# A second layer of 15 products on 2x3x3 blocks, from the ninth output tile on

## The chip, the cores and the metric

One core of a Trainium2 chip runs the whole program. The time is device microseconds (us) of that core; the kernel before takes 1906.94 us, the median of three runs (1906.71 to 1906.95). Engines: PE multiplies matrices into PSUM; VectorE (DVE), ScalarE (ACT) and GpSimd (POOL) do the rest; SyncE (SP) starts transfers. Each engine takes its instructions strictly in the order in which the program holds them, and waits where an input or a buffer is not ready.

## The reference

```python
def reference(x, w_in, w_out):                  # x: (8, 3008, 256) fp32
    X = np.fft.fft(np.fft.fft(x, axis=1), axis=2).real.astype(np.float32)
    h = X.reshape(24064, 256) @ w_in            # w_in: (256, 2048)
    g = np.where(h > 0, h, np.exp(np.minimum(h, 0)) - 1)
    return (g @ w_out).astype(np.float32)       # w_out: (2048, 256)
```

A Fourier transform over sequence and channels, of which the real part is kept, feeds a two-layer network with the activation ELU. Everything is float32.

## The kernel before

The real part of the transform has two mirrored halves, so the kernel works on 12032 columns (rows of the output, transposed), each of which yields two output rows: a "plus" and a "minus" one. The columns are cut into 47 tiles of 256. For a tile and each of 8 steps (`i`), the first layer forms two blocks of 128 hidden channels (`f = 2i, 2i+1`) in a bank `H` of PSUM: `seed` (ACT) puts a rank-one term there, `mm_P` adds the cosine part (2 products), `even_part` (ACT) copies that to `E`, `mm_Q` adds the sine part (2 products). `H` is then the plus side, and `h_minus` (DVE) makes the minus side `2E-H`. ELU takes, for each side, `below` and `exp` on ACT and `elu` (`g_plus`, `g_minus`) on DVE. The results stand in a buffer `G` of one step.

The second layer multiplies `w_out` with these. `sum_1` to `sum_4` (POOL, 256 columns each) and the summed weights `WT` turn the 8 products of a 2x2 by 2x2 block product into 7 (`mm_X1`, `mm_X2`, `mm_X3`) of 256 columns, which accumulate over the tile's 8 steps in four banks, `pA` to `pD`. Per tile four DVE additions (`comb_1`, `comb_2`, `comb_22`, `comb_3`) and an ACT copy (`comb_copy`) rebuild the result, two DVE transposes turn it, and SP stores it. The bank `M` holds the negative part of the minus side. A product is two matmul instructions in the trace, each with its own weight load: fp32 goes through PE in two parts.

Beside this runs the Fourier transform of the next batch element. A batch element spans 47 steps. Its folds and turns are POOL and DVE additions in SBUF (`mirror_sum`, `half_sum`, `channel_fold`, `quarter_pairs`, `turn_pairs`), its matrix products are short (`Quarter.mms`, 94 or 95 columns), use `H` banks too, and DVE unfolds them into rings `Rr` and `Ir` that the first layer reads.

The order is written by hand: each operation is entered with a time (`at(t, fn)`, in steps of `PERIOD`), all are sorted by it, and the recorded order on each engine follows. The times are not kept by the chip; only the order is. The three `H` banks are given out by `bank_H` by those times. A last small part, `mid_*`, computes the one output row of each batch element that the halves leave out; its products with `w_out` stand at the program's end.

Of the kernel before, what the change touches and what calls it, by code (L numbers as in the profile page):

```python
# [177 lines left out]
def kernel(  # L178
# [184 lines left out]
    ebias = cpool.tile([128, 1], FP, tag="ebias")  # L363
    nc.vector.memset(ebias, -896.0 * 2.0**23)
    wide = moe_w_in.dtype == I64
    assert moe_w_out.dtype == moe_w_in.dtype
# [173 lines left out]
        for c in range(8)  # L540
    ]

    MC = {}
    for kodd in range(2):
        for ri in range(2):
# [10 lines left out]
            )  # L556

    QM = {}

    def load_quarter_mats(ri, kodd):  # L560
        t = cpool.tile([128, BW], FP, tag=f"MC{ri}{kodd}", name=f"QM{ri}{kodd}")
        QM[ri, kodd] = t
        n = sum(QW[i % 2] for i in range(2 * ri + kodd))
# [6 lines left out]
    warm = cpool.tile([128, 1], FP, tag="warm")  # L570
# [55 lines left out]
    def vtt(o, a, b, op):  # L626
        pin(nc.vector.tensor_tensor(out=o, in0=a, in1=b, op=op))
# [651 lines left out]
    def ext_side(g, rows=NB):  # L1279
        kodd, par = EXT[g]  # L1280
        n = NO if kodd else NE if par else 2 * NH
        t = spool.tile([128, 384], FP, tag="side", bufs=2, name="side")
        act(t[0:rows, 0:n], state["ext"][32 * g : 32 * g + rows, 0:n])
        state["side", par] = t

# [104 lines left out]
    def even_part(i):  # L1390

        S = steps[i]
        S.E = spool.tile([128, 512], FP, tag="E", bufs=2, name="E")
# [12 lines left out]

    def open_G(S):
        if not hasattr(S, "G"):
            S.G = spool.tile([128, GW], FP, tag="G", bufs=3, name="G")

    def h_minus(i):
        S = steps[i]
        open_G(S)
        pin(
            nc.vector.scalar_tensor_tensor(  # L1415
                out=two(S.G[:, 0:512])[:, :, ::-1], in0=two(S.E), scalar=2.0,
                in1=two(S.H), op0=ALU.mult, op1=ALU.subtract,
            )
        )

    def below(o, h):

# [33 lines left out]
    def g_minus(i):  # L1456
        S = steps[i]
        elu(S.G[:, 0:512], S.G[:, 0:512], S.M)

    def blk(S, j, n=1):  # L1460
        return S.G[:, j * TW : (j + n) * TW]

    def tt_of(i):

        return vtt if i == n_tiles * 8 - 1 else gtt

    def sum_1(i):
        S = steps[i]
# [1 line left out]

    def sum_3(i):
        S = steps[i]
        tt_of(i)(blk(S, 4), blk(S, 2), blk(S, 0), ALU.subtract)

    def sum_2(i):
        S = steps[i]
        tt_of(i)(blk(S, 2), blk(S, 5), blk(S, 0), ALU.subtract)

    def sum_4(i):
        S = steps[i]  # L1480
        tt_of(i)(blk(S, 6), blk(S, 2), blk(S, 1), ALU.add)

    def prod(i, a, half, lhsT, j):
        S, T = steps[i], tiles[i // 8]
# [56 lines left out]

    def comb_copy(q):
        T = tiles[q]
        T.p1 = spool.tile([128, TW], FP, tag="p1", bufs=1, name="p1")
        act(T.p1, T.acc[0][:, 0:TW])

    def plain_v(q):
# [36 lines left out]
        store(q, 0, 1, 0)  # L1584
        store(q, 1, 0, 1)

    def turn_half(q, part):

        T = tiles[q]
        if not part:  # L1590
            T.o = spool.tile([128, 1024], FP, tag="ot", bufs=2, name="ot")
        src = (T.v if part > 1 else T.u)[:, part % 2 * TW : (part % 2 + 1) * TW]
        pin(nc.vector.transpose(out=T.o[:, part * TW : (part + 1) * TW], in_=src))
        store(q, part, *((1, 0), (0, 1), (0, 0), (1, 1))[part])

    def comb_half(q, half):
        T = tiles[q]
        c = slice(half * TW, (half + 1) * TW)
        vtt(T.v[:, c], T.v[:, c], T.acc[3][:, c], ALU.add)

    def turn_v(q):
        T = tiles.pop(q)
        tiles[q, 1] = T
# [6 lines left out]
    def store(q, part, sg, half):  # L1610

        T = tiles[q]
        j, end = q * TW, min((q + 1) * TW, n_cols)
        while j < end:
            b, c = divmod(j, HALF)
            odd, cc = divmod(c, RUN)
# [32 lines left out]


    def mid_mm():
        pm = state["mid"] = bank_H(now[0] + 3 * PERIOD, True)
        for n, (W, R) in enumerate(((Wc, R4), (Ws, Rx4))):
            wv = W.rearrange("p (j g a) -> p g j a", g=4, a=32)
            for g in range(4):
                mm(pm[32 * g : 32 * g + 32, :], R, wv[:, g], n == 0, n == 1)

    def mid_below():
        t = spool.tile([128, HALF + 1], FP, tag="rx", bufs=1, name="mid")
        state["mh"], state["mr"] = t[:, 0:512], t[:, 512:1024]  # L1660
        below(state["mr"], state["mid"])

    def mid_g():
        h, r = state["mh"], state["mr"]
        elu(h, state["mid"], r)
        pin(nc.vector.transpose(out=r, in_=h))

    def mid_out():
        po = state["mo"] = bank_H((total + 2) * PERIOD + 2.8)
        t = state["mr"]  # L1670
        for j in range(NF):
            g = j % 4
            mm(
                po[32 * g : 32 * g + 32, 0:ND],
                t[:, 32 * j : 32 * j + 32],
                w2[:, j * ND : (j + 1) * ND],
                j < 4,
                j >= 12,
            )

    def mid_copy():
        act(state["mh"][:, 0:ND], state["mo"][:, 0:ND])

    def mid_pick():
        po = state["mo"] = bank_H((total + 3) * PERIOD)
        mm(po[0:32, 0:ND], pick[:, 0:32], state["mh"][:, 0:ND], True)

    def mid_store():
        ob = state["mr"][0:NB, 0:ND]
        pin(nc.vector.tensor_copy(out=ob, in_=state["mo"][0:NB, 0:ND]))  # L1690
        nc.sync.dma_start(
            out=bass.AP(
                tensor=out.tensor,
                offset=out.offset + HALF * ND,
                ap=[[SEQ * ND, NB], [1, ND]],
            ),
            in_=ob,
        )

    state = {}  # L1700
# [189 lines left out]
    for i in range(8):  # L1890
        at((12.9 + 0.5 * i) * T + 3.6, lambda i=i: sum_weights(i))
    total = n_tiles * 8
    WINOGRAD = (
        (T + 2.91, sum_1),
        (T + 3.6, sum_3),
# [2 lines left out]
        (2 * T + 0.87, mm_X1),  # L1898
        (2 * T + 3.04, mm_X2),
    )  # L1900
    for slot in range(total):
        i = slot % 2 * 8 + slot // 2 if slot < 16 else slot
        t = slot * T

        X3 = (
            (
                3 * T + 0.1 if i % 8 == 0 else 3 * T + 3.045 if i == total - 2 else 2 * T + 3.05,
                "",
                mm_X3,
            ),  # L1910
# [37 lines left out]
    for q in range(2, n_tiles):  # L1948
        t = (8 * q + 9) * T
        if q == n_tiles - 1:  # L1950
            turns = (
                (4.205, lambda q: turn_half(q, 0)),
                (T + 2.4, lambda q: turn_half(q, 1)),
                (T + 2.5, lambda q: comb_half(q, 0)),
                (T + 2.6, lambda q: turn_half(q, 2)),
                (T + 2.7, lambda q: comb_half(q, 1)),
                (T + 2.8, lambda q: turn_half(q, 3)),
            )
        else:
# [126 lines left out]
    for b in range(2, NB):  # L2086
# [62 lines left out]
    last = total - 40  # L2149
    at(  # L2150
        (last - 8) * T,
        lambda: nc.sync.dma_start(out=Rx4[127:128, 0:NB], in_=r4_dr),
    )
    for n, dt, fn in (
        (last, 4.75, mid_mm),
        (last + 1, 1.46, mid_below),
        (last + 2, 1.6, lambda: exp_neg(state["mr"])),
        (last + 3, 1.0, mid_g),
        (total + 1, 3.3, mid_out),
        (total + 2, 2.75, mid_copy),  # L2160
        (total + 2, 2.91, mid_pick),
        (total + 2, 2.92, mid_store),
    ):
        at(n * T + dt, fn)
    for t, _, fn in sorted(events, key=lambda e: e[:2]):
# [32 lines left out]
```

## Time and profile before

| what | value |
|---|---|
| median of three runs | 1906.94 us |
| the profiled execution | 1907.16 us |
| its span, first to last instruction | 1905.4 us (1.8 us lie around it) |
| granted PE clock | 1.000 |
| busy: PE, DVE, ACT, POOL | 1898.3, 1232.0, 1391.4, 1353.1 us |

The span is one row after another of PE's work. Busy times count an instruction from its start to its end, and PE's instructions overlap, so the distance of their starts is what a product costs. Stretches differ: those with much of the transform's DVE work (about 640 to 760 us, and again every 235 us), those with less, and the end without any.

### The profile page before, as it was taken

What the parts mean: (1) busy time and instruction counts of PE and PEld (TensorE: products, weight loads), DVE (VectorE), ACT (ScalarE), POOL (GpSimd) and SP (SyncE); (2) the same over time, 40 slices, a digit from 0 to 9 for tenths busy, and PEclk for the clock granted to TensorE, in tenths of its full rate; (3) what the DMA queues carried; (4) which work ended last, traced back from release to release, by engine and by line L of the source; (5) the groups of instructions that cost most, each with busy time, mean ns of one, the idle gap of its engine ahead of it and who ended that gap; (6) DMA issues with size and microseconds to landing.
All of it is one profiled execution on the core that took longest, in us unless ns stands there. A gap on an engine that the chain in (4) does not pass through costs nothing.

```text
span 1905.4 us, 28620 instructions
## 1 busy us (share of the span) xinstructions
PE 1898.3 (100%) x8972; PEld 1656.8 (87%) x8972; DVE 1232.0 (65%) x2174; ACT 1391.4 (73%) x2803; POOL 1353.1 (71%) x1846
## 2 busy tenths in 40 slices
PE   9999999999999999999999999999999999999999
PEld 6888888888888888888888888888888888888887
DVE  8755555667666676667766677666776667655445
ACT  5767667777777777777777777777777777777775
POOL 4888658786687766777667777687766777556664
PEclk9999999999999999999999999999999999999999
DMA  8145211211011110211102111022110210100101
GB/s 340 45 33 43 55 24 45 53 24 36 12 44 41 32 33 12 47 40 30 31 19 50 35 27 31 13 56 44 24 24 16 55 21 15 17 12 15 20 11 24
DMA packets 278901, 73.66 MB, mean 39 GB/s; under 512 B 254382, under 2 KB 268972, under 8 KB 278750
## 3 DMA queue, kind: packets, MB, share of 16 engines
q1 hardware_dynamic: 270110, 61.40, 15.9%
q0 software_dynamic: 6464, 10.18, 1.7%
q8 instruction: 71, 1.16, 0.3%
q14 instruction: 80, 0.66, 0.1%
q10 hardware_dynamic: 2176, 0.26, 0.1%
HBM read 46.92 MB, written 24.80 MB: 38 GB/s over the span
## 4 chain that ended last, share of the span: by engine, by line
PE 96%; DVE 2%; ACT 1%; issue 0%; DMA 0%; POOL 0%; ACTq 0%; POOLq 0%; DVEq 0%
PE H L621 37%; PE pB L621 17%; PE pD L621 17%; PE pC L621 17%; PE pA L621 9%; DMA xl<-in_x_dram,ix 0%; DVE e L721 0%; ACT G L633 0%; DVE o L721 0%; POOL w L630 0%; DVE G L1431 0%; DVE E L1401 0%; ACT M L633 0%; ACT E L633 0%; DVE pow L462 0%
## 5 line engine op out<-in xcount | busy, mean ns | idle before, releaser
L630 POOL TENSOR_TENSOR G<-G 128x256 f32<-128x256 f32 x1437 | 1047.4, 737 | 498.0 <-DVE G L1431 358.5
L1431 DVE SCALAR_TENSOR_TENSOR G<-G,H 128x512 f32<-128x512 f32 x376 | 258.2, 687 | 554.5 <-ACT G L633 554.5
L633 ACT ACTIVATE G<-H 128x512 f32<-128x512 f32 x376 | 224.5, 597 | 259.0 <-DVE G L1415 255.4
L621 PE MATMUL H<-Rr,Wsc 128*128 128x256 f32 x1504 | 388.7, 381 | 1.0 <-ACT Wsc L633 0.5
L621 PE MATMUL H<-Ir,Wsc 128*128 128x256 f32 x1504 | 386.7, 380 | 0.7 <-DVE E L1401 0.7
L633 ACT ACTIVATE H<-Rb,wex 128x256 f32<-128x256 f32 x720 | 341.2, 474 | 40.0 <-DVE G L1431 21.5
L621 PE MATMUL pC<-G,WT 128*128 128x256 f32 x1440 | 369.8, 379 | 0.0
L633 ACT ACTIVATE E<-H 128x512 f32<-128x512 f32 x360 | 214.5, 596 | 182.0 <-PE H L621 181.7
L621 PEld LDWEIGHTS H<-Ir,Wsc 128*128 128x128 f32 x1504 | 285.6, 190 | 40.6 <-DVE E L1401 1.5
L621 PEld LDWEIGHTS H<-Rr,Wsc 128*128 128x128 f32 x1504 | 281.7, 190 | 43.1 <-issue 2.3
L621 PEld LDWEIGHTS pC<-G,WT 128*128 128x128 f32 x1440 | 274.2, 190 | 36.6
L1415 DVE SCALAR_TENSOR_TENSOR G<-E,H 128x512 f32<-128x512 f32 x376 | 255.0, 678 | 8.4 <-PE H L621 4.3
L1431 DVE SCALAR_TENSOR_TENSOR G<-M,G 128x512 f32<-128x512 f32 x376 | 256.7, 683 | 0.7 <-ACT M L633 0.7
L633 ACT ACTIVATE G<-G 128x512 f32<-128x512 f32 x376 | 235.0, 625 | 0.0
L621 PE MATMUL pA<-G,w 128*128 128x256 f32 x784 | 229.6, 380 | 0.1
L621 PE MATMUL pB<-G,w 128*128 128x256 f32 x784 | 229.5, 379 | 0.0
L621 PE MATMUL pD<-G,w 128*128 128x256 f32 x784 | 229.4, 379 | 0.0
L633 ACT ACTIVATE M<-G 128x512 f32<-128x512 f32 x376 | 224.4, 597 | 2.8 <-DVE G L1415 2.8
L633 ACT ACTIVATE M<-M 128x512 f32<-128x512 f32 x376 | 222.7, 592 | 0.1
L621 PE MATMUL pB<-G,WT 128*128 128x256 f32 x720 | 214.7, 380 | 0.0
L621 PE MATMUL pD<-G,WT 128*128 128x256 f32 x720 | 214.4, 379 | 0.0
L621 PEld LDWEIGHTS pA<-G,w 128*128 128x128 f32 x784 | 149.2, 190 | 20.6 <-DVE G L1431 0.5
(175 smaller groups left out, 1794.3 us busy)
## 6 DMA issues: line engine op xcount, KB each, us to landing
out_dram<-ot SPq DMA_DIRECT2D x496, 32.0 KB
xq<-in_x_dram SPq DMA_DIRECT2D x48, 94.0 KB
out_dram<-ot SPq DMA_DIRECT2D x256, 2.0 KB
Rb<-r SPq DMA_DIRECT2D x10, 376.0 KB
raw<-in_moe_w_in_dram SPq DMA_DIRECT2D x7, 512.0 KB
MC<-dft_mats SPq DMA_DIRECT2D x3, 943.5 KB
xq<-in_x_dram SPq DMA_DIRECT2D x12, 192.0 KB
xq<-in_x_dram SPq DMA_DIRECT2D x36, 64.0 KB
```

Of the source, the lines that this page charges most:

```text
L621: nc.tensor.matmul(out_, lhsT=lhsT, rhs=rhs, start=start, stop=stop, skip_group_check=True)
L630: pin(nc.gpsimd.tensor_tensor(out=o, in0=a, in1=b, op=op))
L633: pin(nc.scalar.activation(out=o, in_=i, func=func, **kw))
L1415: nc.vector.scalar_tensor_tensor(out=two(S.G[:, 0:512])[:, :, ::-1], in0=two(S.E), scalar=2.0, in1=two(S.H), op0=ALU.mult, op1=ALU.subtract,)
L1431: nc.vector.scalar_tensor_tensor(out=o, in0=e, scalar=-1.0, in1=h, op0=ALU.add, op1=ALU.max)
```

## The change

The first 8 tiles stay. From the ninth on (`NEW = 8`, 39 tiles) the second layer works on other blocks:

- The 512 columns of a hidden block (256 minus, 256 plus) lie side by side in a ring `GG` of 8 such blocks. Its first and last column are set aside (`keep_ends`, four small DVE copies per tile); the 510 left are three runs of 170 (`BL`).
- Three hidden blocks make a group; five groups and one single block are the 16. A group is a product of 2x3 weight blocks with 3x3 column blocks, 18 products done as 15 with sums. The single block takes 6. So a tile has 81 products of 170 columns where it had 56 of 256. They accumulate in five banks: `pA` to `pD` and `M`, three regions in each.
- Per group 8 sums stand ahead of the products (`group_sum`): `A1` to `A4`, `S3`, `S4` on POOL, `S1`, `S2` on DVE, some over 340 columns at once. The single block has two (POOL).
- 37 summed weight blocks (`make_combo`) are made once, in steps 61 to 70, by turns on POOL and DVE; they lie in free parts of buffers of the transform and in the old `WT`.
- The outputs take 19 operations per tile (`out_sum`): 15 on DVE, 2 on ACT, 2 on POOL, in place of four on DVE and one on ACT.
- `below_minus` now writes into `H` in place of `M`, so that an `H` bank is held until `g_minus`. `E` has one buffer from that tile on.
- The columns set aside, with those of `mid`, are 86 (`NS`) and take 16 products of 256 columns at the end (`single_mm`) and one store; the `mid` products at the end go.
- Each operation of a tile has its own time in a table `TILE_AT`, the same for all 39 tiles. The transform's times stay.

```diff
+NEW = 8
+BL = 170
+NS = 2 * (NP - NEW) + 8
...
+    def new_below_minus(i):
+        S = steps[i]
+        below(two(S.H), S.m)
...
+    def keep_ends(i):
...
+        pin(nc.vector.tensor_copy(out=o, in_=b[:, :, 0:512:511]))
...
+        tt = vtt if name in ON_DVE else gtt
+        if name == "A1":
+            tt(F(0, 1), B(7, 5), B(8, 6), ALU.add)
+        elif name == "A2":
+            tt(F(2, 1), F(0, 1), B(5, 8), ALU.add)
+        elif name == "A3":
+            tt(F(6), B(0), B(2), ALU.add)
+        elif name == "S1":
+            tt(F(4, 3), B(0, 2), B(1, 6), ALU.subtract)
+        elif name == "A4":
+            b3 = B(3)
+            tt(F(5, 6), F(4, 6), pair_of(b3, 0), ALU.add)
+        elif name == "S2":
+            tt(F(4, 7), F(4, 5), B(6, 4), ALU.subtract)
+        elif name == "S3":
+            tt(F(0), B(2), F(0), ALU.subtract)
+        elif name == "S4":
+            tt(F(7), F(7), F(2), ALU.subtract)
+
+    ON_DVE = ("S1", "S2")
...
+            W = wblock((g,), WPLAIN[p]) if p in WPLAIN else wcombo((g,), p)
+            M = gb(g, PLAIN[p]) if p in PLAIN else fb(5 * (q - NEW) + g, FORM[p])
+        mm(region(p), W, M, not g and j % 3 == 0, g == 5)
...
+        if name == "D0":
+            act(tmp(2), R(9))
+        elif name == "D1":
+            vtt(cb(u, 0), tmp(2), R(11), sub)
+        elif name == "D2":
+            vtt(tmp(0), R(8), tmp(2), sub)
...
+        elif name == "E5":
+            gtt(cb(u, 0, 2), cb(u, 0, 2), tmp(1, 2), add)
...
+        elif name == "E7":
+            vtt(cb(v, 1), cb(v, 1), cb(v, 0), add)
+        elif name == "E8":
+            vtt(cb(v, 0, 2, 2 * BL), cb(v, 0, 2, 2 * BL), regions(7, 15), add)
...
+    def single_mm(f):
+        if not f:
+            state["single"] = bank_H((total + 30) * PERIOD)
+        mm(
+            state["single"][0:NS, 0:ND],
+            single(f),
+            w2[:, f * ND : (f + 1) * ND],
...
+    TILE_AT = {
+        "seed": (
+            -3.840, -0.624, 2.855, 5.507, 15.632, 16.480, 23.562, 26.176,
...
+        t = 61.0 + 0.25 * n
...
+        at(t * T + 1.3, lambda gs=gs, p=p, n=n: make_combo(gs, p, gtt if n % 2 else vtt))
+    for q in range(NEW, n_tiles):
+        new_tile(q)
...
-    for slot in range(total):
+    for slot in range(8 * NEW):
```

What the order becomes is shown at three places. First PE in a tile of the steady part, where `H<-Rr` and `H<-Ir` are the first layer's products and `p...<-G` those of the second. Before:

```order
L621 MATMUL H<-Rr,Wsc 128x256 x2
L621 MATMUL pA<-G,w_68 128x256
L621 MATMUL pB<-G,w_68 128x256
L621 MATMUL pB<-G,WT_903 128x256
L621 MATMUL H<-Ir,Wsc 128x256 x2
L621 MATMUL pC<-G,WT_904 128x256
L621 MATMUL pC<-G,WT_902 128x256
L621 MATMUL pD<-G,WT_905 128x256
L621 MATMUL pD<-G,w_68 128x256
L621 MATMUL H<-Rr,Wsc 128x256 x2
```

Now, with `GG` the ring, `F` the sums, and `QM_...`, `WT_...` the weight sums:

```order
L639 MATMUL H<-Rr,Wsc 128x256 x2
L639 MATMUL pD<-GG,QM_2548 128x170
L639 MATMUL M<-GG,QM_2312 128x170
L639 MATMUL pC<-F,QM_2452 128x170
L639 MATMUL pD<-F,QM_2452 128x170
L639 MATMUL pA<-GG,WT_875 128x170
L639 MATMUL pD<-F,QM_2548 128x170
L639 MATMUL H<-Ir,Wsc 128x256 x2
L639 MATMUL pC<-F,w_68 128x170
L639 MATMUL pA<-GG,QM_2452 128x170
L639 MATMUL M<-F,QM_2548 128x170
L639 MATMUL M<-GG,w_68 128x170
```

The regular round of 4 and 7 products per step is gone: products of several groups are mixed, and more of them stand between two parts of the first layer.

Second, DVE where it also has the transform's half sums (`xq<-xq,xq`). Before (L1431 `elu`, L1415 `h_minus`):

```order
L1415 SCALAR_TENSOR_TENSOR G<-E,H 128x2x256
L627 TENSOR_TENSOR xq_11050<-xq_11042,xq_11110 96x256 x2
L1431 SCALAR_TENSOR_TENSOR G<-G,H 128x512
L1431 SCALAR_TENSOR_TENSOR G<-M,G 128x512
L1415 SCALAR_TENSOR_TENSOR G<-E,H 128x2x256
L627 TENSOR_TENSOR xq_11118<-xq_11042,xq_11110 96x256 x2
L1431 SCALAR_TENSOR_TENSOR G<-G,H 128x512
```

Now, in such a place of the new part (L1455 `elu`, L1488 `new_h_minus`; `F<-GG` and `GG<-GG` of 2x170 are `S1`, those of 340 `S2`; a group's sums lie in `F` or in the ring's tail by turns):

```order
L1455 SCALAR_TENSOR_TENSOR GG<-H,GG 128x2x256
L1488 SCALAR_TENSOR_TENSOR GG<-EE,H 128x2x256
L645 TENSOR_TENSOR xq_6476<-xq_6580,xq_6660 94x256 x2
L645 TENSOR_TENSOR GG<-GG 128x340
L645 TENSOR_TENSOR F<-GG 128x2x170
L1455 SCALAR_TENSOR_TENSOR GG<-GG,H 128x2x256
L1488 SCALAR_TENSOR_TENSOR GG<-EE,H 128x2x256
L1526 COPY SS<-GG 128x4x2
L1455 SCALAR_TENSOR_TENSOR GG<-GG,H 128x2x256
L645 TENSOR_TENSOR xq_6543<-xq_6580,xq_6660 94x256 x2
L645 TENSOR_TENSOR F<-F,GG 128x340
```

Sums of two SBUF operands now stand between the activations on DVE, beside the transform's own.

Third, PE at the program's end. Before:

```order
L621 MATMUL pC<-G,WT_902 128x256
L621 MATMUL pD<-G,WT_905 128x256
L621 MATMUL pD<-G,w_68 128x256
L621 MATMUL pD<-G,WT_905 128x256
L621 MATMUL pD<-G,w_68 128x256
L621 MATMUL H<-w_68,mid 32x256 x16
L621 MATMUL H<-mid,pick 32x256
```

Now:

```order
L639 MATMUL pD<-GG,WT_878 128x170
L639 MATMUL pD<-F,WT_877 128x170
L639 MATMUL M<-GG,WT_875 128x170
L639 MATMUL pD<-GG,WT_875 128x170
L639 MATMUL M<-F,WT_878 128x170
L639 MATMUL H<-w_68,SS 86x256 x12
L639 MATMUL H<-w_68,CC 86x256 x4
L639 MATMUL M<-WT_875,w_68 128x170 x2
L639 MATMUL pD<-WT_875,w_68 128x170
```

The 16 products of the columns set aside come ahead of the last tile's last three products, and nothing of `mid` comes behind them.

More of the change, by code (lines that the diff above doesn't have):

```diff
@@ L1392, in even_part @@
         S = steps[i]
-        S.E = spool.tile([128, 512], FP, tag="E", bufs=2, name="E")
+        S.E = next_of("E", EE, 512, 1 if i >= 8 * NEW else 2)
         if S.seeded:
@@ L1458, in g_minus, with new_h_minus, new_below_plus, new_exp_plus @@
         elu(S.G[:, 0:512], S.G[:, 0:512], S.M)
+    def new_h_minus(i):
+        S = steps[i]
+        S.m, S.p = slots(i)
+        pin(
+            nc.vector.scalar_tensor_tensor(
+                out=S.m[:, :, ::-1], in0=two(S.E), scalar=2.0,
+                in1=two(S.H), op0=ALU.mult, op1=ALU.subtract,
+            )
+        )
+    def new_below_plus(i):
+        S = steps[i]
+        S.m, S.p = slots(i)
+        below(S.p, two(S.H))
+    def new_exp_plus(i):
+        exp_neg(steps[i].p)
@@ new lines, in out_tiles, with cb, tmp @@
+    def out_tiles(q):
+        T = tiles[q] = Tile()
+        if "uv" not in state:
+            state["uv"] = [
+                spool.tile([128, 512], FP, tag=t, bufs=1, name=t) for t in "uv"
+            ]
+            for t in state["uv"]:
+                pin(nc.vector.memset(t[:, 0:512:511], 0.0))
+        T.u, T.v = state["uv"]
+    def cb(t, n, m=1, step=BL):
+        v = t[:, 1 + BL * n : 1 + BL * (n + 1)]
+        return v if m == 1 else pair_of(v, step)
+    def tmp(n, m=1):
+        v = EE[:, 512 + BL * n : 512 + BL * (n + 1)]
+        return v if m == 1 else pair_of(v, BL)
@@ L1460, in blk, with new_turn @@
+    def new_turn(q, part):
+        T = tiles[q]
+        if not hasattr(T, "o"):
+            T.o = spool.tile([128, 1024], FP, tag="ot", bufs=2, name="ot")
+        c = 512 * part
+        pin(nc.vector.transpose(out=T.o[:, c : c + 512], in_=(T.u, T.v)[part]))
+        store(q, 2 * part, 1, part)
+        store(q, 2 * part + 1, 0, part)
     def blk(S, j, n=1):
         return S.G[:, j * TW : (j + n) * TW]
-    def tt_of(i):
-        return vtt if i == n_tiles * 8 - 1 else gtt
     def sum_1(i):
@@ L1585, in turn_u @@
         store(q, 1, 0, 1)
[L1587 to L1599, printed above, removed]
     def turn_v(q):
@@ L1893 @@
+    at((total + X0 + 1) * T, single_store)
     WINOGRAD = (
```

360 lines of the change are left out of this document (305 added, 55 removed), and 9 rows, old and new, of the table TILE_AT.

## The prediction

> **What bounds the kernel now.** I read the page's busy times and chain first, then windows, then shapes and the timeline where a price was needed.
>
> ```profile
> PE 1898.3 (100%) x8972; PEld 1656.8 (87%) x8972; DVE 1232.0 (65%) x2174; ACT 1391.4 (73%) x2803; POOL 1353.1 (71%) x1846
> ...
> PE 96%; DVE 2%; ACT 1%; issue 0%; DMA 0%; POOL 0%; ACTq 0%; POOLq 0%; DVEq 0%
> ```
>
> PE never rests, and the chain that ended last is PE for 96%. So less PE work is worth its full length as long as nobody else becomes late. Three windows show who could: one with much of the transform on DVE, one with less, one with none.
>
> ```profile
> core 0: us, PE busy (x) PEld busy (x) DVE busy (x) ACT busy (x) POOL busy (x), PEclk, DMA share, GB/s
> 640.00:760.00 120.00, 120.00 (x589) 106.51 (x588) 85.68 (x167) 87.95 (x180) 82.92 (x116) 1.00 0.12 25
> 758.00:875.00 117.00, 117.00 (x543) 103.24 (x543) 73.57 (x114) 88.41 (x179) 92.62 (x126) 1.00 0.18 40
> 1740.00:1880.00 140.00, 140.00 (x650) 123.55 (x649) 69.06 (x112) 105.51 (x210) 85.36 (x119) 1.00 0.09 14
> ```
>
> DVE is busy for 71%, 63% and 49%: the transform takes 22 points of it in the first.
>
> **PE's gain.** What a product costs is the distance of two starts.
>
> ```profile
> 1606.78 0.60 PE L621 MATMUL pD<-G,WT 128*128 128x256 f32 x2
> 1607.21 0.59 PE L621 MATMUL pD<-G,w 128*128 128x256 f32 x2
> 1607.64 0.36 PE L621 MATMUL H<-QM,e 95*128 95x95 f32 x2
> 1607.84 0.39 PE L621 MATMUL H<-QM,o 94*128 94x95 f32 x2
> 1608.06 0.39 PE L621 MATMUL H<-QM,e 94*128 94x95 f32 x2
> 1608.29 0.39 PE L621 MATMUL H<-QM,o 94*128 94x94 f32 x2
> 1608.51 1.06 PE L621 MATMUL H<-Rr,Wsc 128*128 128x256 f32 x4
> ```
>
> A product of 256 columns takes 0.432 us (0.43 from start to start), one of 94 or 95 takes 0.22. For 170 I need the slope, from the shapes' mean times:
>
> ```profile
> L621 PE MATMUL pA<-G,w 128*128 128x256 f32 x784 | 229.6, 380 | 0.1
> L621 PE MATMUL H<-MC,eo 128*128 128x376 f32 x16 | 5.7, 479 | 0.0
> L621 PE MATMUL H<-MC,eo 128*128 128x188 f32 x8 | 1.6, 323 | 0.0
> L621 PEld LDWEIGHTS H<-QM,e 94*128 94x128 f32 x192 | 27.2, 192 | 1.2
> ```
>
> From 188 to 256 columns an instruction grows by 57 ns, from 256 to 376 by 99: 0.83 ns a column both times. So 170 columns take 86 x 0.83 = 71 ns less than 216, that is 145 ns, and a product 0.289 us. Below that the short products show a floor of 0.11 us per instruction, which 145 ns clears. Per tile 56 x 0.432 = 24.2 us become 81 x 0.289 = 23.4: 0.8 us, over 39 tiles 31 us. With the first layer's 32 products (13.8) a tile then asks 37.2 us of PE.
>
> Those short products also judge a rule. The Trainium skill, "Trainium Kernel Development and Optimization", section Best Practices, says to judge distance to roofline by LDWEIGHTS busy time, not by matmul busy time. By the 190 ns that a load lasts, the change, with 50 more loads per tile, would make PE the slower; that is the third rival below. The rows differ: four loads of 192 ns each went by in 2 x 0.22 us, so a load's duration is not what it blocks.
>
> **The program's end.**
>
> ```profile
> 1898.91 0.60 PE L621 MATMUL pD<-G,w 128*128 128x256 f32 x2
> 1899.44 1.93 PE L621 MATMUL H<-w,mid 128*32 128x256 f32 x32
> 1902.11 0.62 PE L621 MATMUL H<-mid,pick 128*32 128x256 f32 x2 [0.74 <-ACT mid L633]
> 1903.20 0.29 SPq L1691 DMA_DIRECT2D out_dram<-mid  x1
> ```
>
> The 16 new products take 16 x 0.432 = 6.9 us of PE; 1.93 + 0.62 = 2.5 go: +4.4. Behind PE's last second-layer product stood some 6 us (1899.5 to 1905.4: `mid`, its copies, its store). Now, after `x13` and `x7` of the single block, DVE's chain E2, E4, E6, E7, E8 and two transposes stand there, near 3.5 us by the rows below, and a store: the same length. The last tile has no next tile's first layer to fill PE while its last sums are made: +1 (0 to +3).
>
> **DVE, the cover that may fail.** The prices:
>
> ```profile
> L627 DVE TENSOR_TENSOR u<-p,pB 128x512 f32<-128x512 f32 x45 | 30.6, 681 | 0.4 <-PE pB L621 0.4
> L627 DVE TENSOR_TENSOR u<-v,pC 128x256 f32<-128x256 f32 x45 | 18.9, 420 | 1.5
> L627 DVE TENSOR_TENSOR xq<-xq,xq 96x256 f32<-96x256 f32 x48 | 37.5, 817 | 0.0
> L627 DVE TENSOR_TENSOR Rr<-bs,H 128x376 f32<-128x376 f32 x2 | 1.0, 542 | 1.0 <-PE H L621 1.0
> L627 DVE TENSOR_TENSOR bs<-H,anti 128x188 f32<-128x188 f32 x3 | 1.0, 348 | 3.4 <-ACT anti L633 3.4
> L627 DVE TENSOR_TENSOR R<-bs,H 128x1 f32<-128x1 f32 x7 | 1.0, 149 | 0.0
> L1431 DVE SCALAR_TENSOR_TENSOR G<-G,H 128x512 f32<-128x512 f32 x24 | 16.4, 685 | 24.4 <-ACT G L633 24.4
> ```
>
> The last row is that of the window 640 to 760: 24 steps, three tiles of 40 us, so a tile there has 85.68 / 3 = 28.6 us of DVE. In the end window a tile (38 us) has 0.49 x 38 = 18.6. The transform's share in a busy tile is thus 10.0, in a lighter one (0.63 x 38 = 23.9) 5.3.
>
> Of the 18.6 the old sums go: three of 0.68 and one of 0.42, less overlap, 2.4. What comes:
> - S1, S2, ten per tile, 340 columns, both operands in SBUF. Alone 0.51 (between 348 ns for 188 and 542 for 376). The half sums, which are of this kind, take 817 ns for 256 columns where 420 is the price with one operand in PSUM. So up to 0.90 for 340. I take 0.70: 7.0 (5.1 to 9.0).
> - 13 output sums of 170 from PSUM and E7: 14 x 0.33 = 4.6. E8 (340): 0.5.
> - Four copies of 8 elements: 0.15 each by the one-column row, up to 0.4 if they wait: 0.8.
>
> 18.6 - 2.4 + 12.9 = 29.1 us per tile (27 to 32). PE gives it 37.2 in the end part: ample. In a lighter tile it is 34.4 of 37.2. In a busy tile it is 39.1, and PE there needs 40 - 0.8 = 39.2: level. That is the place that decides. A queue at its limit loses time, but what waits for DVE has some room: after `mm_Q`, the next use of that `H` bank needs `h_minus`, `below_minus`, `exp_minus`, `g_minus` and two `seed`s, and PE's order puts its own work between. The prices are the 685 ns above and these:
>
> ```profile
> L633 ACT ACTIVATE M<-G 128x512 f32<-128x512 f32 x376 | 224.4, 597 | 2.8 <-DVE G L1415 2.8
> L633 ACT ACTIVATE H<-Rb,wex 128x256 f32<-128x256 f32 x720 | 341.2, 474 | 40.0 <-DVE G L1431 21.5
> ```
>
> That is 2 x 0.69 + 2 x 0.6 + 2 x 0.47 = 3.5 us; the fifth step's `mm_P` stands some 6 us of PE work behind the third's `mm_Q` (counted in the new order), so 2 to 2.5 us are left. The first products of a group have more. I take 0.4 us lost per busy tile (0 to 2), 120 us in each 235 us, six times, 18 tiles: 7 us. Lighter tiles: none (0 to 0.5 each).
>
> **POOL and ACT.**
>
> ```profile
> L630 POOL TENSOR_TENSOR G<-G 128x256 f32<-128x256 f32 x1437 | 1047.4, 737 | 498.0 <-DVE G L1431 358.5 <-PE H L621 82.0
> L630 POOL TENSOR_TENSOR WT<-w 128x128 f32<-128x128 f32 x16 | 7.8, 485 | 0.0
> L630 POOL TENSOR_TENSOR o<-e,o 94x384 f32<-94x384 f32 x12 | 12.0, 997 | 0.0
> L633 ACT ACTIVATE p<-pA 128x256 f32<-128x256 f32 x45 | 17.1, 379 | 1.6 <-PE pA L621 1.6
> ```
>
> POOL's 32 x 0.737 = 23.6 per tile become 16 of 340 (0.91) and 18 of 170 (0.57), 24.8; with the transform's 4 (82.92 / 3 less 23.6) 29 of 39: hidden. ACT loses one copy of 0.38 and gets two of about 0.3: hidden at 105.5 / 140 = 75%. `below_minus` into `H` instead of `M` costs the same 597 ns; what it holds longer is the bank, counted above. SP's queue loses and gains a few stores: nothing. The 37 weight sums, about 13 us of DVE and POOL each within 43 us of a busy stretch where both already run at 70%, fill both up: +2 (0 to +4).
>
> How POOL and DVE disturb each other is to be read from four POOL sums without and with two half sums beside them:
>
> ```profile
> 1891.05 3.02 POOL L630 TENSOR_TENSOR G<-G 128x256 f32<-128x256 f32 x4 [1.74 <-DVE G L1431]
> ...
> 762.59 3.15 POOL L630 TENSOR_TENSOR G<-G 128x256 f32<-128x256 f32 x4 [0.80 <-DVE G L1431]
> ...
> 763.56 1.60 DVE L627 TENSOR_TENSOR xq<-xq,xq 96x256 f32<-96x256 f32 x2
> ```
>
> POOL loses 0.13 us to two DVE sums; DVE pays 1.60 for 0.84. So it is DVE that pays.
>
> **Sum** against the profiled execution's 1907.2 us (0.2 above the median): 1907.2 - 31 + 4.4 + 1 + 2 + 7 = 1890.6, say 1890.
>
> **Rivals.**
> 1. No stall: DVE's S sums near 0.51, 37 us in a busy tile. 1907.2 - 31 + 4.4 + 1 = 1882. For it: PE idles nowhere before; against it: DVE's sum without room. Chance 0.30.
> 2. Slower: DVE becomes the bound in the busy tiles, since each S waits out POOL's running sum (0.90), each copy too. Then 32 + 10 = 42 against 39.2: 2.8 x 18 = 50, so 1932. It decides from 1882 + 25, that is 1.4 us per busy tile, or 40.6 us of DVE. For it: the half sums' 817 ns. Against: in busy tiles POOL rests for 31%, and S2 follows a POOL sum that has just ended. Chance 0.22. The Trainium skill, "SBUF — State Buffer", section Who interferes with whom, has two SBUF operands on DVE and POOL's reads exclude each other for whole instructions, which speaks for it; by the trace POOL loses far less than that.
> 3. The weight load rules PE: 226 loads x 0.190 = 42.9 us per tile against 38.0 now, x 39 = +191, near 2100. The 0.22 us pitch speaks against it. Chance 0.02.
> 4. It doesn't do what it says: losses of 22 to 29 us eat the gain, within 0.2% (3.8 us, about what a measurement of this kernel can tell from no change): a mild form of 2. Chance 0.12.
> 5. The likeliest, the sum above, with 3 to 20 us of stalls: 1884 to 1902. Chance 0.34.
>
> Faster: 0.30 + 0.34 - 0.02 for its upper edge = 0.62; same 0.12; slower 0.26 with that edge and 3. Range 1873 to 1928: below, a gain of 37 (170 columns in pure proportion to 256: 0.287) and no loss at the end; above, most of rival 2. The likeliest's own range is 1876 to 1903.
>
> **What would show it.** In the trace after: matmuls of 170 columns 145 ns apart (right) or 190 (rival 3); S1, S2 at 0.6 to 0.8 us on DVE (0.9 and more: rival 2); PE's busy share in windows like 640 to 760 at 97 to 100%, its idle there put down to DVE; POOL under 80%. I am wrong if PE idles in the end window, where DVE has 8 us to spare, since then the order itself, a bank or a ring slot, makes PE wait.

## The result, and the profile after

The changed kernel takes 1927.5 us (median; 1926.85 to 1927.9), the kernel before 1906.95: a ratio of 1.0106 (1.0088 to 1.0123). It is some 20 us slower where 17 us faster was forecast. The time lies at the upper edge of the stated range (1873 to 1928), but that edge stood there for another cause, rival 2, so that it lies inside is luck. Its profiled execution took 1927.36 us, with a span of 1925.6.

The page's busy times, the summary of the chain that ended last, and PE's two largest waits:

```profile
PE 1884.2 (98%) x10920; PEld 1744.3 (91%) x10920; DVE 1553.0 (81%) x3165; ACT 1441.3 (75%) x2843; POOL 1362.2 (71%) x1945
...
PE 84%; DVE 10%; ACT 2%; issue 1%; POOL 1%; DMA 1%; ACTq 0%; SPq 0%; DVEq 0%; POOLq 0%
...
PE pD L639 <- DVE v L645: 11.4, 5, 2.3
PE H L639 <- ACT EE L651: 4.4, 4, 3.1
```

PE's share of the chain fell from 96% to 84%, and DVE now holds 10%. PE's own work did shrink. Laid end to end at the distances that their starts show (144 ns for 170 columns, 216 for 256, the short ones at their floor of 110), PE's instructions come to 1894.1 us before (1.9 of it the `mid` products) and 1867.1 after: 27.0 less. The rest is told by the starts of PE's instructions, what each leaves open beyond its price, summed by stretch:

| where the time went, us | before | after | difference |
|---|---|---|---|
| PE's instructions end to end | 1894.1 | 1867.1 | -27.0 |
| PE open in the first 360 us | 2.8 | 5.1 | +2.3 |
| PE open at 360 to 480 us (old order meets new) | 0.1 | 8.9 | +8.8 |
| PE open around five places (588, 822, 1058, 1294, 1530 us, 20 us to each side) | 0.0 | 19.7 | +19.7 |
| PE open elsewhere | 4.3 | 7.8 | +3.5 |
| from PE's last instruction to the span's end | 3.0 | 15.8 | +12.8 |
| sum | | | +20.1 |

The windows of the changed kernel, with the same columns as before: the busy stretch, one of the five places, and the end part.

```profile
640.00:760.00 120.00, 119.69 (x746) 114.06 (x745) 107.02 (x243) 92.21 (x185) 84.56 (x126) 1.00 0.13 25
...
800.00:840.00 40.00, 37.61 (x216) 35.15 (x215) 32.53 (x58) 28.41 (x55) 26.89 (x41) 0.96 0.18 37
1800.00:1840.00 40.00, 40.00 (x243) 37.78 (x242) 30.68 (x65) 32.25 (x63) 24.14 (x37) 1.00 0.09 15
```

Where DVE is fullest (107 of 120) PE loses 0.3 us in 120. It loses 2.4 in 40 where DVE has 7 to spare. So the loss in the steady part isn't DVE's load. One row of DVE and the POOL rows beside it show what it is, at the second of the five places:

```profile
820.75 3.97 DVE L645 TENSOR_TENSOR v<-v 128x170 f32<-128x170 f32 x1
824.64 0.68 DVE L1455 SCALAR_TENSOR_TENSOR GG<-H,GG 128x512 f32<-128x512 f32 x1
...
820.42 0.81 POOL L648 TENSOR_TENSOR u<-u,EE 128x170 f32<-128x170 f32 x1
821.19 1.64 POOL L648 TENSOR_TENSOR F<-F,GG 128x340 f32<-128x340 f32 x2
822.80 0.48 POOL L648 TENSOR_TENSOR GG<-GG 128x170 f32<-128x170 f32 x1
823.24 0.79 POOL L648 TENSOR_TENSOR u<-u,EE 128x340 f32<-128x340 f32 x1
823.98 0.54 POOL L648 TENSOR_TENSOR F<-GG,F 128x170 f32<-128x170 f32 x1
```

`E7` (`v<-v`, 170 columns), one of the output sums, lasts 3.97 us and ends when POOL, which ran six sums without a pause, has stopped. `E8` stands behind it on DVE, and the next tile's first `pD` product on PE needs `E8`. The view of the buffer `v` gives least, median and greatest duration (ns) over all 39 tiles:

```profile
L645 DVE TENSOR_TENSOR v<-pA,EE x39: 329/329/331, 421.2 to 1900.9; 128x170 f32<-128x170 f32 x39
L645 DVE TENSOR_TENSOR v<-v x39: 320/325/3973, 430.9 to 1910.8; 128x170 f32<-128x170 f32 x39
```

The sum with an operand in PSUM (`pA`) hardly varies, though POOL runs beside 38 of its 39. `E7`, with both operands in SBUF, takes some 325 ns in 33 tiles, 0.65 us in the last and 3.97 us in five.

Why five tiles, and not all, can be read from a tile without the loss:

```profile
862.16 0.50 DVE L645 TENSOR_TENSOR GG<-GG 128x340 f32<-128x340 f32 x1
862.58 0.32 DVE L645 TENSOR_TENSOR v<-v 128x170 f32<-128x170 f32 x1
...
861.32 0.55 POOL L648 TENSOR_TENSOR u<-u,EE 128x170 f32<-128x170 f32 x1
862.83 1.66 POOL L648 TENSOR_TENSOR GG<-GG 128x340 f32<-128x340 f32 x2 [0.96 <-DVE GG L645]
```

Here `E3` (POOL, `u<-u,EE` of 170 columns) has ended, POOL waits for DVE's group sum, and `E7`, which stands right behind that sum, gets in before POOL starts again. It is so in all 33 tiles: POOL idles as `E7` starts. In the five, 1.2 us of the transform's sums (`xq<-xq,xq`) stand on POOL just ahead of `E3`, `E3` still runs as `E7` starts, and the sums behind it start without a wait.

### The profile page after: what moved, and what is told of

Same layout as the page of the kernel before. It is cut to its first block, busy times and chain, and to the rows that moved or that the text cites. A ratio compares the mean times of both kernels' runs of the same rounds, so it can differ in the third digit from the quotient of the medians.

```text
span 1925.6 us, 34720 instructions
## 1 busy us (share of the span) xinstructions
PE 1884.2 (98%) x10920; PEld 1744.3 (91%) x10920; DVE 1553.0 (81%) x3165; ACT 1441.3 (75%) x2843; POOL 1362.2 (71%) x1945
## 4 chain that ended last, share of the span: by engine, by line
PE 84%; DVE 10%; ACT 2%; issue 1%; POOL 1%; DMA 1%; ACTq 0%; SPq 0%; DVEq 0%; POOLq 0%
PE H L639 33%; PE pD L639 12%; PE pC L639 11%; PE pB L639 10%; PE pA L639 9%; PE M L639 9%; DVE v L645 2%; DVE GG L1455 2%; ACT H L651 1%; DVE EE L645 1%; DVE CC L1526 1%; ACT GG L651 1%; DVE GG L1488 1%; DVE GG L645 1%; DVE e L929 0%
## 5 line engine op out<-in xcount | busy, mean ns | idle before, releaser
L648 POOL TENSOR_TENSOR GG<-GG 128x340 f32<-128x340 f32 (+2 forms) x774 | 547.1, 718 | 306.3 <-DVE GG L645 138.7
L1455 DVE SCALAR_TENSOR_TENSOR GG<-GG,H 128x512 f32<-128x512 f32 x376 | 256.8, 683 | 124.7 <-ACT GG L651 119.6
L651 ACT ACTIVATE EE<-H 128x512 f32<-128x512 f32 x360 | 213.4, 593 | 174.3 <-PE H L639 122.8
L651 ACT ACTIVATE GG<-H 128x512 f32<-128x512 f32 x376 | 223.7, 595 | 159.4 <-PE H L639 71.6
L1488 DVE SCALAR_TENSOR_TENSOR GG<-EE,H 128x512 f32<-128x512 f32 x312 | 212.6, 682 | 86.3 <-PE H L639 47.4
L1455 DVE SCALAR_TENSOR_TENSOR GG<-H,GG 128x512 f32<-128x512 f32 x312 | 212.4, 685 | 69.2 <-ACT H L651 64.4
L651 ACT ACTIVATE GG<-GG 128x512 f32<-128x512 f32 x376 | 235.8, 627 | 8.5
L648 POOL TENSOR_TENSOR F<-F,GG 128x340 f32<-128x340 f32 x196 | 164.2, 850 | 79.1 <-DVE F L645 77.2
L651 ACT ACTIVATE H<-GG 128x512 f32<-128x512 f32 x312 | 185.3, 594 | 41.6 <-DVE GG L1455 39.7
L651 ACT ACTIVATE H<-H 128x512 f32<-128x512 f32 x312 | 179.7, 576 | 4.6
```

Source lines behind the costliest of these rows:

```text
L648: pin(nc.gpsimd.tensor_tensor(out=o, in0=a, in1=b, op=op))
L651: pin(nc.scalar.activation(out=o, in_=i, func=func, **kw))
L1455: nc.vector.scalar_tensor_tensor(out=o, in0=e, scalar=-1.0, in1=h, op0=ALU.add, op1=ALU.max)
L1488: nc.vector.scalar_tensor_tensor(out=S.m[:, :, ::-1], in0=two(S.E), scalar=2.0, in1=two(S.H), op0=ALU.mult, op1=ALU.subtract,)
```

## The experiments

The kernel before ran beside each and took 1906.9 to 1907.0 us. Ratios are to it.

| edit of the changed kernel | median us | ratio (95% interval) |
|---|---|---|
| none | 1927.5 | 1.0106 (1.0088 to 1.0123) |
| E7 on POOL | 1913.0 | 1.0032 (1.0020 to 1.0045) |
| set-aside products last | 1923.9 | 1.0090 (1.0073 to 1.0107) |
| weight sums spread | 1927.4 | 1.0108 (1.0091 to 1.0125) |
| all three | 1909.2 | 1.0012 (1.0003 to 1.0022) |
| E7 with an operand in PSUM | 1966.1 | 1.0310 (1.0294 to 1.0326) |
| longer POOL run beside E7 | 1919.6 | 1.0065 (1.0049 to 1.0080) |
| whole stores | 1927.3 | 1.0109 (1.0094 to 1.0125) |
| PSUM operand, whole stores, shorter end | 1960.1 | 1.0279 (1.0265 to 1.0293) |
| pause behind E3 | 1911.8 | 1.0026 (1.0017 to 1.0036) |
| pause, whole stores, shorter end | 1907.05 | 0.9998 (0.9989 to 1.0007) |
| the same, three queues evenly | 1904.8 | 0.9988 (0.9979 to 0.9997) |
| the same, weight sums on POOL | 1908.0 | 1.0008 (0.9999 to 1.0017) |

**E7 on POOL.**

```diff
-            vtt(cb(v, 1), cb(v, 1), cb(v, 0), add)
+            gtt(cb(v, 1), cb(v, 1), cb(v, 0), add)
```

> Only E7 (one sum of 170 columns, both operands in SBUF) moves from DVE to POOL. In the trace after, E7 lasts 3.97 us five times, once per batch element, while POOL runs six sums without a gap; PE then waits 2.45 us for E8 and its clock falls to 0.5 for some us. Theory (the shared port keeps E7 out): the five waits and the cold clock behind them go, 5 x (2.45 + 2) = 22 us, so about 1906 us, granted clock 1.00 from 500 to 1880 us. Rival (DVE and the order are too loaded there, E7 is only where it shows): a wait of like length turns up behind another DVE or POOL operation, and the time stays within 6 us of 1927.5.

All five waits for `v` are gone and the time fell by 14.5 us, less than the 22 of the theory. A new wait came up, the longest near 833 us:

```profile
PE pC L639 <- POOL GG L648: 2.4, 2, 2.0
```

**The set-aside products last.** (`X0` is their time in the order, in steps.)

```diff
-X0 = 2.6
+X0 = 3.6
```

> Only the 16 products of the columns set aside and their store move behind the last tile's last three products. Theory (the end chain E2 to the last store waits 7 us behind them on PE): the last transposes start 7 us earlier; but 27 stores of the set-aside rows then share the queues with the 32 of the tile, so 4 to 7 us are won: 1921 to 1924 us. Rival (the end is set by the issue of the stores, not by PE): within 1.5 us of 1927.5.

3.6 us less, within what was expected. The 6.9 us of products no longer stand ahead of the last tile's last three, but the span still ends 12 us behind PE: the stores remain.

**The weight sums spread.**

```diff
-        t = 61.0 + 0.25 * n
-        if gs[0] == 3:
-            t = max(t, 66.5 + 0.15 * (n - 24))
+        t = 57.2 + 0.35 * n
+        if gs[0] >= 3:
+            t = 66.5 + 0.25 * (n - 24)
```

> Only the 37 weight sums are entered over 57.2 to 69.5 steps in place of 61 to 70: the first 24 start earlier and lie farther apart. In the trace after, PE loses 8 us between 360 and 440 us, where it lost nothing before. Theory (the sums crowd DVE and POOL there): 3 to 7 us are won, 1920 to 1924 us. Rival (what is lost there is the new order meeting the old at the eighth tile, whatever the sums do): within 1.5 us of 1927.5.

No change in time. PE's longest wait in the transition fell from 3.1 to 1.3 us, but the stretch from 320 to 440 us still lost 7.0 us in place of 8.3.

**All three together.**

> The three edits together. If they cost independently, their gains add: 22 + 5 + 5, so about 1895 us, below the 1906.9 of before. If the waits only move, the time stays above 1907.

1909.2, far from the 1895 expected: 18.3 us of the 20 are back. The gains do add (14.5 + 3.6 + 0.1); each was smaller than expected.

**E7 with an operand in PSUM.**

```diff
+    def v0_to_psum(q):
+        act(region(14), cb(tiles[q].v, 0))
...
-            vtt(cb(v, 1), cb(v, 1), cb(v, 0), add)
+            vtt(cb(v, 1), cb(v, 1), R(14), add)
...
+        at(t0 + 58.9, lambda: v0_to_psum(q))
```

> E7 stays where it stands on DVE, but one of its two operands now comes from PSUM: ACT copies E6's result into the region of product 14, which is free by then (one more ACT operation of 0.3 us per tile), and E7 adds from there. Nothing else changes. Theory: what keeps E7 out for 3.97 us is that both its operands lie in SBUF while POOL runs six sums without a gap; with one in PSUM it takes 0.33 us in all five places, PE's five waits of 2.45 us go, and with them the clock's dips: 1927.4 - 14.4 (what E7 on POOL saved) = 1913, 1910 to 1915. Rival: E7 waits there for something else in its place of the order, a result or a semaphore; then it lasts 3.97 us again and the time stays at 1927.

Half right. `E7` lasted 332 to 334 ns in every tile, and POOL was running as it began in 38 of the 39. But the time rose to 1966, because the cure made a wait of its own:

```profile
DVE v L645 <- ACT pD L651: 81.9, 39, 3.9
PE pD L639 <- DVE v L645: 46.7, 38, 1.5
```

ACT's copy stands in ACT's order behind work that waits for PE. `E7` waits for it 2.1 us in every tile, and PE for `E8` 1.2 us in 38. The operand is what decides, but one more engine in a chain that PE waits for cost some 54 us (1966.1 less the 1911.8 of the pause below) where some 15 were won.

**A longer POOL run beside E7.**

```diff
             gtt(cb(u, 0, 2), cb(u, 0, 2), tmp(1, 2), add)
+            if q in (12, 18, 24, 30, 36):
+                for n in range(2):
+                    gtt(tmp(0, 2), pair_of(w2[:, 0:BL], BL), pair_of(w2[:, 512 : 512 + BL], BL), add)
```

> E7 as in the changed kernel, but in tiles 12, 18, 24, 30 and 36 alone POOL makes two sums more of 340 columns (of weights, into a buffer nobody reads) between E5 and S3, inside its run without a gap. Theory: DVE gets in only where POOL pauses, so E7 lasts as much longer as the run: 3.97 + 2 x 0.82 = 5.6 us in five places, PE's wait there grows from 2.45 to about 4.1, five times 1.65 plus a longer time at the low clock: 1934 to 1940. Rival: DVE's stay is set by something of fixed length (4 us), or POOL lets DVE in after a fixed number of sums; then E7 lasts 3.97 and the time is 1927 to 1929.

Neither: `E7` got shorter and the kernel 7.9 us faster. PE's five waits are 1.95 us in place of 2.45, and no fall of its clock follows them (see the end).

```profile
819.62 3.47 DVE L645 TENSOR_TENSOR v<-v 128x170 f32<-128x170 f32 x1
...
822.12 0.78 POOL L648 TENSOR_TENSOR u<-u,EE 128x340 f32<-128x340 f32 x1
822.97 1.89 POOL L648 TENSOR_TENSOR EE<-w 128x340 f32<-128x340 f32 x2
```

The sums that I added write where `E5` had read, so the first of them waits for `E5`'s end. In the records POOL's sums otherwise start some 34 ns before the one ahead has ended; here 78 ns lie between (end at 833.483, start at 833.561 in the trace's own clock, which is 822.896 and 822.974 from the span's start). `E7` came in at that pause, one POOL sum earlier. So the run that was meant to become longer became shorter. Whether a longer run without a pause keeps `E7` out still longer was not tried; the pause itself was, two experiments below.

**Whole stores.** A tile of 255 columns goes out as 7 blocks of 32 and a rest: 32 transfers in place of 16. Here the set-aside column goes out too, with zeros that the program's last store writes over.

```diff
-        j, end = q * TW, min((q + 1) * TW, n_cols) - int(q >= NEW)
+        j, end = q * TW, min((q + 1) * TW, n_cols) - int(q == NP - 1)
```

> Only the stores change: from the ninth tile to the last but one all 256 columns go out (the set-aside column carries zeros there, and the last store of the program writes over them), so that a tile's store is 16 transfers again and not 32. Theory: SP gives out a transfer in about 0.45 us, so the pieces cost SP some 7 us per tile, but in the changed kernel POOL waited for the transform's loads for 2.4 us in all; alone this changes little: 1925 to 1927.5, with SP's wait ahead of the loads gone. Rival: the late loads are also what disturbs the places where E7 stands out or the transition at 360 to 440 us; then the waits of 2.45 us or the transition's 8 us shrink and the time is 1912 to 1922.

As expected, no change by itself. What it moves is a load of the next batch element on SP's queue. The changed kernel first, then this one:

```profile
799.88 26.82 SPq L1889 DMA_DIRECT2D out_dram<-ot  x54
826.79 0.64 SPq L342 DMA_DIRECT2D xq<-in_x_dram  x1
```

```profile
799.57 12.81 SPq L1889 DMA_DIRECT2D out_dram<-ot  x19
812.48 0.64 SPq L342 DMA_DIRECT2D xq<-in_x_dram  x1
```

SP gives out a store piece in about 0.5 us (26.82 for 54), so the load left 14 us later with the pieces. In the changed kernel POOL, held up elsewhere, waited for such loads for 2.4 us in all.

**PSUM operand, whole stores and a shorter end.** Besides the two edits above: `X0 = 3.6`, the set-aside rows copied by DVE and given out by POOL and SP behind the tile's own stores.

> Three edits at once: E7 with an operand in PSUM; whole stores; and a shorter end: the 16 products of the set-aside columns behind the last tile's products (X0 = 3.6), their copy on DVE, their store behind the tile's own and given out by POOL and SP in place of SP and ACT. Theory: the losses are separate, so the gains add: 14.4 for E7, 3.4 for POOL's wait for a load at about 832 us, that stands alone once E7's is gone, 3.5 for the products' place (as measured) and 2 to 4 for the stores at the end: 1927.4 - 14.4 - 3.4 - 6.5 = 1903, 1900 to 1907; a little under the kernel before. Rival: where one wait goes another shows, as when E7 went to POOL: 1908 to 1915, not faster than before.

The rival, and worse: the wait for ACT is in every tile here too (46.8 us). Against the PSUM operand alone, stores and end brought 6.0 us of the 9.9 expected of them.

**A pause behind E3.**

```diff
             gtt(cb(u, 2), cb(u, 2), tmp(0), add)
+            gtt(tmp(0)[:, 0:1], w2[:, 0:1], w2[:, 1:2], add)
```

> E7 stays on DVE, with both operands in SBUF, at its place. New is one POOL sum of a single column behind E3, which writes over a column that E3 has read and so waits for E3's end: POOL has to pause there for some 80 ns, as it did in the run with the longer POOL stretch (833.483 to 833.561 in its records), where E7 came in at just that pause. Theory: DVE's sum gets in at the first pause of POOL, however short. Then E7 lasts 0.7 to 1.0 us in the five places in place of 3.97, PE's five waits of 2.45 go, and the time is 1911 to 1916; POOL's wait for a late load near 830 us may show, as with E7 on POOL (3 us). Rival: DVE gets in only when POOL's work is used up or after a fixed time; then E7 lasts 3.9 to 4.2 and the time is 1927 to 1929.

```profile
817.95 0.68 DVE L645 TENSOR_TENSOR v<-v 128x170 f32<-128x170 f32 x1
...
817.62 0.81 POOL L648 TENSOR_TENSOR u<-u,EE 128x170 f32<-128x170 f32 x1
818.50 0.19 POOL L648 TENSOR_TENSOR EE<-w 128x1 f32<-128x1 f32 x1
818.65 1.66 POOL L648 TENSOR_TENSOR F<-F,GG 128x340 f32<-128x340 f32 x2
```

Right. A POOL sum of one column, with a dependency, brings `E7` from 3.97 to 0.68 us in the five tiles and the kernel 15.7 us. Nothing else on DVE, PE or ACT was touched. In the changed kernel, with the longer POOL run and here, in all fifteen places, `E7` ends 193 to 199 ns after the POOL sum that stands ahead of the pause (with the longer run at 822.896, `E7` at 823.092; here at 818.424 and 818.622), however many sums ran before. The late load is now seen (POOL's waits, and its own row):

```profile
POOL xq L648 <- DMA xq<-in_x_dram: 13.7, 4, 5.1
...
829.15 0.89 POOL L648 TENSOR_TENSOR xq<-xq,xq 94x255 f32<-94x255 f32 x2 [5.12 <-DMA xq<-in_x_dram]
```

POOL holds group sums behind that load, and PE lost 4.2 us around 832.

**Pause, whole stores, shorter end.** `X0 = 3.6`, the copy on DVE, the last stores given out by SP, ACT and POOL in turn.

> The pause behind E3, whole stores (tiles 9 to 46), the 16 products of the set-aside columns behind the last tile's (X0 = 3.6), their copy on DVE, and the stores of the last tile and of the set-aside rows given out by SP, ACT and POOL in turn. Theory: five separate losses, so that the gains add: 14 for E7, 3 for POOL's wait for a late load (none is left with whole stores), 3.5 for the products' place, 2 to 4 for three queues at the end: 1927.4 - 23.5 = 1904, 1900 to 1907, a little under the kernel before. Rival: another wait comes up where those went, as in every cure so far: 1908 to 1915.

1907.05, level with the kernel before and just above the range expected. POOL's waits for loads of `xq` and PE's at the five places are gone. The set-aside rows went to ACT and POOL, 13 each, and SP, which had one, was idle from 1895.2 us on.

**The same, three queues evenly.**

> As the run with the pause behind E3, whole stores and the shorter end, but the 27 stores of the set-aside rows go to the three queues evenly. There ACT and POOL had 13 each, given out until 1900.5 us, while SP had nothing left from 1895.2 on; 9 each at some 0.43 us end near 1897. Theory: the end is set by what the queues give out, so the time falls by 2.5 to 3.5: 1904 (1903 to 1905.5), faster than the kernel before by 0.15%. Rival: the last transfers' landing or a wait on POOL sets the end; then 1906 to 1907.

1904.8 us, within the range expected: 0.12% under the kernel before (0.03 to 0.21%), so level or a little faster, and 22.7 us faster than the change as made. Its end, from the last tile's transposes on, and then that of the changed kernel:

```profile
1887.75 0.67 DVE L1728 STREAM_TRANSPOSE ot<-v 128x512 f32<-128x512 f32 x1
1887.86 4.97 ACTq L1892 DMA_DIRECT2D out_dram<-ot  x10
1892.19 0.42 DVE L1949 COPY single<-H 86x256 f32<-86x256 f32 x1 [3.77 <-PE H L639]
1894.97 4.45 SPq L1968 DMA_DIRECT2D out_dram<-single  x8
```

```profile
1909.48 4.37 SPq L1963 DMA_DIRECT2D out_dram<-single  x13
1912.57 0.67 DVE L1727 STREAM_TRANSPOSE ot<-v 128x512 f32<-128x512 f32 x1
1914.37 8.35 SPq L1889 DMA_DIRECT2D out_dram<-ot  x16
```

In the changed kernel 27 + 32 transfers are given out by two queues behind PE's last product, until 1922.7. That, and not the sums, is the long end.

**The same, weight sums on POOL.**

```diff
-make_combo(gs, p, gtt if n % 2 else vtt)
+make_combo(gs, p, gtt)
```

(and the times of the spread sums)

> As the one with three even queues, and all 37 weight sums on POOL (none on DVE), at steps 57.2 to 70 in place of 61 to 70. It asks what the transition at 360 to 440 us waits for, where PE lost 7.9 us and DVE was busy for 9.52 and 10.00 of 10 us at 380 to 400. Theory: DVE is at its limit there through the weight sums (19 of them, about 16 us of DVE, many held back by POOL); without them PE's loss there falls to 2 to 4 us and the time by 4 to 6: 1899. Rival: the meeting of the two orders makes PE wait, or POOL, busy for 8.3 to 9.8 of 10 there, is late with its sums instead; then PE loses 7 us or more there as before and the time is 1904 or above.

The rival, its second half. Windows of 10 us at the transition, the changed kernel and then this one, and this one's waits:

```profile
380.00:390.00 10.00, 6.89 (x36) 5.70 (x36) 9.52 (x17) 7.02 (x14) 8.33 (x14) 1.00 0.10 30
390.00:400.00 10.00, 9.56 (x58) 8.70 (x56) 10.00 (x14) 5.63 (x12) 9.22 (x13) 1.00 0.21 32
```

```profile
380.00:390.00 10.00, 8.71 (x45) 7.45 (x46) 7.80 (x14) 8.12 (x17) 9.92 (x15) 1.00 0.27 80
390.00:400.00 10.00, 7.66 (x42) 6.79 (x41) 6.89 (x10) 6.48 (x13) 10.00 (x15) 0.94 0.19 29
...
PE pC L639 <- POOL F L648: 2.5, 2, 2.3
PE pB L639 <- POOL GG L648: 1.9, 3, 0.8
PE H L639 <- ACT EE L651: 1.5, 2, 1.3
```

DVE was relieved (10.00 to 6.89) and PE's wait for `EE` fell from 4.4 to 1.5 us, but most of that came with the times: the spread sums alone, with DVE still busy for 9.31 and 9.69 of 10 us there, had brought it to 2.0. That DVE's load caused that wait is not shown. POOL is full instead (9.92 and 10.00), and PE waits for its sums. Against the same kernel without this edit the time is 3.2 us longer. No place of the weight sums that was tried brought time; where they would fit, stays open.

## Why the prediction was wrong, point by point

- **PE's gain and the added products:** right. -31 + 4.4 = -26.6 was forecast, -27.0 is what the starts give. A product of 170 columns is two instructions that start 144 ns apart, so 0.288 us (the window 1800 to 1840 holds 243 instructions, first-layer ones included, without a gap). The third rival, by which weight loads set PE's pace, is out by the same number: its two loads of 0.19 us would have asked for 0.38.
- **The place that decides:** wrong place. The busy stretch was to be level for DVE and lose 7 us; it loses 0.3 in 120. DVE has 107.0 us of work there in some three tiles, about 35 a tile against 39.1 forecast. The group sums on DVE took 0.605 us, under the 0.70 taken:

```profile
L645 DVE TENSOR_TENSOR GG<-GG 128x340 f32<-128x340 f32 x194 | 117.4, 605 | 0.5
```

- **"14 x 0.33" and "lighter tiles: none":** the step that failed, by the most. `E7` was priced like 13 sums with an operand in PSUM, and DVE's danger was read from its load. It lies in one instruction with both operands in SBUF that PE waits for soon after. Five of them cost 19.7 us of PE, 15.7 by the pause behind `E3`. It is not the whole miss: with it cured the kernel still takes 1911.8. Of the 37 us between 1890 and 1927.5 it has 19.7, the end 12.8, the transition 6.8 beyond its 2 and the first 360 us 2.3; the 8 us put on busy tiles and on the last one came to 3.5 in all. The trace of before held the mechanism; its view of the buffer `xq` gives the half sums (both operands in SBUF) and the sums with an operand in `H`:

```profile
L627 DVE TENSOR_TENSOR xq<-xq,xq x96: 414/836/951, 245.9 to 1545.8; 96x256 f32<-96x256 f32 x48, 94x256 f32<-94x256 f32 x48
L627 DVE TENSOR_TENSOR xq<-H,near x54: 245/249/258, 434.5 to 1677.4; 128x94 f32<-128x94 f32 x30, 127x94 f32<-127x94 f32 x12, 128x95 f32<-128x95 f32 x6, 127x95 f32<-127x95 f32 x6
```

  The kind decides: the second varies by 13 ns, the first from 414 to 951. Its bound of about one POOL sum came from POOL's order, not from the kind. `sum_2` writes over what `sum_3` reads, `sum_4` reads what `sum_2` wrote, and in the records such a sum starts 78 or 79 ns after the end of the one ahead, also where no half sum is near (1892.460 to 1892.538). All 89 half sums that lasted over 0.6 us end 277 to 285 ns after a POOL sum that such a pause follows. From 420 us on POOL has 602 such pauses in the kernel before and one in the changed kernel. With the pauses went the bound.
- **"So it is DVE that pays":** right in direction, read from a sum over four sums; the merged row of four POOL sums at 762.59 hides the two pauses (764.006 to 764.084, 764.880 to 764.958) in which the two half sums got in. Rival 2 had the mechanism (a sum that waits out POOL) but not where: it charged every S, which were mostly spared (0.605 us on average against 0.90), in the busy tiles.
- **The Trainium skill's rule beside rival 2**, "SBUF — State Buffer", section Who interferes with whom: a DVE sum with two SBUF operands contends with POOL's reads, one with a single SBUF operand does not. The trace agrees on both (320 to 3973 ns, against 329 to 331). Its sentence that the first gets the port for the whole instruction, written there for DVE's two-port modes, would hold `E7` for one POOL sum, 0.85 us; here it was held over several, until POOL paused.
- **The program's end, "the same length":** wrong by 10 us, and the 2.5 us of `mid` were counted twice: as gone from PE (+4.4, not +6.9), and as a part of the 6 us that stay. 5.9 us lay behind the last second-layer product, now 15.7. The sums and transposes were counted (3.5), but not the 32 + 27 transfers, at 0.3 to 0.5 us each on two queues.
- **"SP's queue loses and gains a few stores: nothing":** wrong. 16 stores a tile became 32, more where a batch element ends in it. It shows only when `E7`'s wait is gone: 4.2 us around 832, gone with whole stores.
- **The weight sums, +2:** 8.8 us with all that meets at 360 to 480, over the bound of 4. The new order's first tile adds its own sums there, and DVE is at 9.5 to 10.0 of 10, POOL at 8.3 to 9.2; which of these makes PE wait is not settled by the two edits that moved the sums.
- **The first 360 us, not counted:** +2.3: the same 1600 products start 2.3 us later, 1.9 of it within the first 40 us. PE idles there for 2.0 us before, 5.0 in the changed kernel and 2.9 to 4.7 in the edits, none of which touches that part. Its cause was not sought.
- **"What would show it":** every sign named there came as the forecast had it (matmuls 144 ns apart, `S` sums of 0.605 us, PE busy for 119.69 of 120 us, POOL at 71%, no idle PE in the end window), and the time was still wrong. All of them were means or loads of a stretch; none would have shown five single instructions.

## What to carry to other kernels

Before you move work to an engine, list the instructions that it can't start while a neighbour runs, by where their operands lie, and ask for each what waits behind it; load by stretch doesn't show them. A pause in the neighbour's run was cheap protection here; an operand from PSUM protects too, but it cost more than it won where it brought another engine into the chain. Look also at what pauses the old order had, for a new order may lose them. Count transfers as instructions of their queue, and look at what stands behind them, above all at the program's end.

## What was not expected of the hardware

- A DVE sum of 170 columns, 0.32 us alone, was kept out for 3.97 us, in five tiles alike within 5 ns; a pause of POOL of about 80 ns was enough to let it in (3.47 and 0.68 us).
- PE's clock after those waits. Windows of 3 us around 822 in the changed kernel:

```profile
821.00:824.00 3.00, 2.50 (x14) 1.96 (x12) 3.00 (x1) 1.73 (x3) 3.00 (x6) 1.00 0.20 32
824.00:827.00 3.00, 1.21 (x7) 1.21 (x8) 3.00 (x6) 0.57 (x2) 0.53 (x2) 0.93 0.13 18
827.00:830.00 3.00, 3.00 (x11) 2.73 (x10) 1.13 (x3) 2.01 (x5) 1.84 (x3) 0.50 0.27 87
```

  The granted clock falls to 0.50, and 11 matmuls pass where some 18 should (243 in 40 us). The traces of four runs with these waits (this kernel, set-aside products last, weight sums spread, whole stores) hold 20 of 2.45 us, 2.67 from start to start; 12 were followed by such a fall, which lasts 3.41 us and costs some 1.7. Of three waits of 2.2 us (`E7` on POOL, all three, pause behind `E3`) two were, of five of 1.95 us (the longer POOL run) none. So in that run the 0.5 us by which the waits were shorter brought more than their own length. The Trainium skill, "TensorE: Matmul & The Clock Gate", section HAM oscillation — how this bites in real kernels, gives the rule as no idle gap of PE above some 3.4 us; here a wait of 2.2 us was enough twice and one of 2.45 us in 12 of 20.
